# Retention attention feeding a mixture of experts: score products in half rows, and three loads that change place

## The chip, the cores and the metric

The kernel runs on one core of one Trainium2 chip. The metric is the time of one execution on the device in microseconds (us). For the kernel before, three runs took 440.48, 441.44 and 442.04 us; the median is 441.44.

A core has a matrix engine (TensorE, shown as PE for its products and PEld for the weight loads that go ahead of them), VectorE (DVE), ScalarE (ACT), GpSimd (POOL) and SyncE (SP). SP, ACT and POOL also ask for transfers between main memory and the core; sixteen DMA engines carry them. Each engine works through its own list of instructions in the order in which it is written, and waits at an instruction whose inputs aren't there.

## The reference

Two blocks, one after the other, all in 32-bit floats. The first is a retention recurrence over 4 batches, 8 heads, 768 tokens and heads of 64:

```python
gamma = 1.0 - 2.0 ** (-5.0 - np.arange(H))
scale = 1.0 / np.sqrt(D)
for t in range(S):
    state = gamma * state + np.einsum('bhd,bhe->bhde', k[:, :, t], v[:, :, t])
    y[:, :, t] = scale * np.einsum('bhd,bhde->bhe', q[:, :, t], state)
```

Its output, 3072 rows of 512, goes into a mixture of 8 experts in which each row is sent to the one expert with the highest logit:

```python
logits = x @ w_gate
expert_idx = np.argmax(logits, axis=1)
gate_w = softmax(logits)[arange(N), expert_idx]
for e in range(E):                       # the rows of expert e
    h = np.maximum(x_sorted[lo:hi] @ w1[e], 0.0)
    y_sorted[lo:hi] = h @ w2[e]
out = gate_w[:, None] * y                # back in the order of the tokens
```

w1 is 8 x 512 x 1024, w2 8 x 1024 x 512 (2 MB for each expert in each).

## The kernel before

**Attention in chunks.** The recurrence is worked in chunks of 128 tokens. Within a chunk there are products of scores (k against q, under a causal mask) and of the masked scores with v; across chunks a state of 64 x 64 per head is carried. The decay is put into q and v beforehand by element-wise products with a table (`scale_q`, `scale_v`: lines 606 and 611). There are STEPS = 12 steps (lines 906 on); a step handles one chunk for two batches, and steps 0 and 2 and so on (the even ones) begin a pair of chunks that share one load of q of 512 KB per batch. k and v are loaded per step and batch, 256 KB each. Step s does, in the order that is written by hand for every engine:

- asks for the loads of later steps (ACT for q; SP for k and v of step s + 3), and scales q and v for coming steps on POOL;
- `scores` for both batches (line 650). A tile `sc[j]` holds for one parity j of the head four pairs of heads. Each head's product is 64 x 128 x 128 and is split in two here, over c, so that a quadrant of 64 x 64 of the matrix engine is used by each: four products, two parities j and two halves c, fill the array. DVE masks them (line 655);
- products of the carried state with q (`with_state`, line 674, 64 x 64 quadrants);
- for the even following step, transposes of q (`turn_q`, line 617, copied by ACT, line 630, called from `ahead_q` in odd steps), and for every following step transposes of k (`turn_k`, line 617, copied by ACT, line 636, called from `ahead`);
- the rows of the step before are turned on DVE (`to_rows`, line 716) and stored by SP to `x_d` in main memory (`store`, line 723); logits (lines 734 to 745);
- the new state (`next_state`, line 687) and the products of masked scores with v (`within`, line 705), copied by ACT (lines 708 and 711).

**Loads at the start.** Before the loop SP asks for q, k and v of step 0, k of step 1, q and k of step 2, v of step 1 and v of step 2, in this order. v of step 1 is scaled partly by POOL in step 0 (batch 1) and partly by DVE in step 1 (batch 0). From step 1 on, ACT asks for one 512 KB load of q at the start of every step until step 8: the first batch of a pair in odd steps, the second in even ones.

**Routing beside attention.** From steps 5 and 9 on and after the last step, `place` works out which expert each token belongs to and its rank there, in pieces that are threaded into the steps (`WHEN`). After the second of them, in step 10, the rows known so far for expert 0 are gathered from `x_d` by POOL (`gather`, line 174) into `xs2[0]`. Right behind these gathers POOL sets one element of the tile for expert 0's w1 (line 839). As the load of that part of the tile writes the same element, SP can ask for it (line 158) only after the gathers have been issued. The load comes in two halves of 1 MB over the columns of w1, each called from step 10, with the store of step 9 between them.

**The experts.** `layer1` (line 233) runs expert 0's first layer for 256 rows, one block of 128 columns of w1 at a time; further routing is worked out between the blocks, and the remaining rows are gathered. From 148 us on the experts follow densely: most products are those of line 333.

Of the kernel before, what the change touches and what calls it, by code (L numbers as in the profile page):

```python
# [13 lines left out]
F32 = mybir.dt.float32  # L14
# [7 lines left out]
P = 128  # L22
# [31 lines left out]
def kernel(  # L54
# [11 lines left out]
    nc = tc.nc  # L66
    B, H, S, D = q.shape
# [85 lines left out]
        nc.sync.dma_start(w1t, w1v[:, ds(e, 1), :, :])  # L153
        return w1t

    def half_of_weights1(w1t, e, i):

        nc.sync.dma_start(w1t[:, :, :, ts(i, F // 2)], w1v[:, ds(e, 1), :, ts(i, F // 2)])

    def weights2(pool, e, parts=1):  # L160
        w2t = pool.tile([P, 1, FT, DM], F32, tag="w2t", name="w2t")
# [406 lines left out]
    with ExitStack() as actx:  # L568
# [19 lines left out]
        def load(nm, s, b, parts=1, by=nc.sync):  # L588
            m, b1, e = where[s]
            src = {"q": q, "k": k, "v": v}[nm]  # L590
            if nm == "q":
                to = att.tile([P, H, 2 * D], F32, tag=nm, name=nm, bufs=4)
                for part in (ts(i, H // parts) for i in range(parts)):
                    by.dma_start(to[:, part, :], src[2 * b1 + b, part, ts(m, 2 * P), :].rearrange(
                        "h (t e) d -> t h (e d)", e=2))
            else:
                to = att.tile([P, H, D], F32, tag=nm, name=nm, bufs=8)
                nc.sync.dma_start(to, src[2 * b1 + b, :, ts(2 * m + e, P), :].rearrange("h t d -> t h d"))
            raw[nm, s, b] = to

        def scale_q(s, b, by=nc.gpsimd, parts=1):
# [7 lines left out]
        def scale_v(s, b, by=nc.gpsimd):  # L609
            vs = att.tile([P, H, D], F32, tag="vs", name="vs", bufs=4)  # L610
            by.tensor_tensor(out=vs, in0=raw.pop(("v", s, b)), op=ALU.mult,  # L611
                             in1=inner(dec[:, ts(NC + 2 * where[s][0] + where[s][2], H)], D))
            raw["vs", s, b] = vs
# [28 lines left out]
        def scores(s, b):  # L642
            kT, qT = front.pop((s, b)), q_of(s, b)
            sc = [pairs_of("sc", 4, "sc") for _ in range(2)]
            am = [att.tile([P, HP, P], F32, tag=f"am{j}", name=f"am{j}") for j in range(2)]
            for a in range(HP):
                for c in range(2):
                    for j in range(2):
                        r = ts(j, D)
                        nc.tensor.matmul(sc[j][ts(c, D), a, :], lhsT=kT[r, a, ts(c, D)], rhs=qT[r, a, :],  # L650
                                         start=True, stop=True)

            def mask():
                for j in range(2):
                    nc.vector.tensor_tensor(out=am[j], in0=sc[j], in1=middle(causal[:, :], HP), op=ALU.mult)  # L655

            return am, mask
# [93 lines left out]
        def place(i):  # L751
# [82 lines left out]
            if i == NR - 2:  # L834
                head = inv[:, :, 0 : TC + HALF]
                src, far = sources(head, "_e")
                gather(xs2[0], src[:, 0:TC], range(HALF), 2 * NEXT[i + 1] * P)
                wa.append(first.tile([P, 1, DT, F], F32, tag="w1t", name="w1t"))
                nc.gpsimd.memset(wa[0][:, 0, 0, 0:1], 0.0)
                early.extend([head, far, src])  # L840

        def pad_ranks(at):
# [9 lines left out]
        def load_all(nm, s):  # L852
            for b in range(2):
                load(nm, s, b)
# [8 lines left out]
        load("q", 2, 0)  # L863
        load_all("k", 2)
        load("q", 2, 1)
        load_all("v", 1)
        load_all("v", 2)
        ctx.enter_context(tc.manual_schedule(engines={PE, ACT, POOL, DVE, SP}))
        xTa = first.tile([P, DT, EARLY], F32, tag="xTa", name="xTa")
# [32 lines left out]
        def step(s, at):  # L902
            for _ in range(WHEN.get(s, "").count(at)):
                next(rest, None)

        for s in range(STEPS):
            n = s + 2 + s % 2
            if 2 < n < STEPS:
                load("q", n, 1 - s % 2, by=nc.scalar)
            if s + 3 < STEPS:  # L910
                load_all("k", s + 3)
                if s == 7:
                    store(5)
                if s + 4 < STEPS:
                    load_all("v", s + 3)
            if s == 0:
                scale_q(2, 0)
                scale_q(2, 1)
                scale_v(1, 1)
            elif s + 2 < STEPS:  # L920
                if s % 2 and s > 1:
                    scale_q(s + 1, 1)
                for b in range(2):
                    scale_v(s + 1, b)
                if s % 2 == 0:
                    scale_q(s + 2, 0)
            if s in (1, 2):
                nc.gpsimd.memset(xs2[s % 2], 0.0)
            if s:
                am = [scores(s, b) for b in range(2)]  # L930
                am[0][1]()
                step(s, "m")
                if s + 2 != STEPS:
                    am[1][1]()
            y = outputs()
            if s + 1 == STEPS:
                logit = logits([s - 2, s - 1])
                rows_in_order()
            if where[s][0] or where[s][2]:
                with_state(s, y)  # L940

            def ahead():
                for b in range(2):
                    turn_k(s + 1, b)

            def ahead_q():
                if s % 2:
                    for b in range(2):
                        turn_q(s + 1, b)

            if s:
                if s + 1 < STEPS:
                    if s % 2:
                        logit = logits([s - 1] if s == 1 else [s - 2, s - 1])
                    ahead()
                reduce = logits_of(*logit) if s % 2 else lambda: None
                step(s, "p")
                if s + 2 == STEPS:
                    am[1][1]()
                    for b in range(2):  # L960
                        scale_v(s + 1, b)
                if s + 1 < STEPS:
                    ahead_q()
                to_rows(s - 1)
                reduce()
                if s == 1:
                    scale_v(1, 0, nc.vector)
                if s == NEXT[NR - 1] + 1:
                    half_of_weights1(wa[0], 0, 0)
                if s != 6:  # L970
                    store(s - 1)
                if s + 1 == STEPS:
                    wa.append(weights2(first, 0, 2))
                if s == NEXT[NR - 1]:
                    load_all("v", STEPS - 1)
                if s == NEXT[NR - 1] + 1:
                    half_of_weights1(wa[0], 0, 1)
                if s in NEXT:
                    rest = chain(rest, place(NEXT.index(s) - 1))
                step(s, "a")  # L980
            next_state(s)
            if s == 0:
                ahead()
            step(s, "b")
            if s + 1 == STEPS:
                pad_ranks(acc[:, NR - 1, 0:2])
            step(s, "r")
            within(s, y, am, early_rows if s + 1 == STEPS else lambda: None)
            step(s, "c")
# [319 lines left out]
```

## Time and profile before

| what | value |
|---|---|
| median of the runs (range) | 441.44 us (440.48 to 442.04) |
| profiled execution | 441.59 us, of which the span on the core is 439.9 us |
| PE busy in the span | 417.8 us (95%), 3979 products |
| PEld (weight loads) | 384.8 us (87%) |
| DVE, ACT, POOL busy | 244.1, 129.6 and 251.9 us |
| score products (line 650) | 768, 24.2 us busy |
| TensorE clock granted, mean | 0.994 |
| DMA over the span | 85.44 MB, 194 GB/s mean |

The span runs from the first to the last instruction on the core; the profiled execution is 1.69 us longer than its span. A 32-bit product stands in the profile as two records, and so does its weight load; that is why 32 calls of a step's scores show as 64. A row of a timeline gives start, time, engine, line, operation, output and inputs, the count of merged instructions, and in brackets how long the engine had been idle before it and what ended that. A row of the groups gives busy time and mean nanoseconds of one, and then the idle time before. Stretches give the busy time of each engine with the count of its instructions, then the granted clock, the mean busy share of the sixteen DMA engines and GB/s. A share a little over 1 can occur, since packets overlap on an engine.

### The profile page before, as it was taken

The page shows a single profiled execution, that of the slowest core. Times are in us where ns is not written, and L with a number is a line of the kernel's source. Part 1 is how long each engine was busy: PE and PEld are TensorE (multiplying, and loading weights), DVE is VectorE, ACT ScalarE, POOL GpSimd, SP SyncE. Part 2 cuts the span into 40 slices and gives each one's busy share as a digit, 9 for nine tenths or more (in the row PEclk, how much of TensorE's full clock was granted, in tenths as well). Part 3 has the DMA queues.
Part 4 walks back from the last instruction along what each step waited for, and adds up shares of the span by engine and source line. Part 5 has one row for each costly group of instructions (what it writes and reads, how often), then busy time and mean ns, then how long its engine had stood idle before and what let it go on. Part 6 is the DMA issues. An engine that isn't in the chain of part 4 may idle for free.

```text
span 439.9 us, 10496 instructions
## 1 busy us (share of the span) xinstructions
PE 417.8 (95%) x3979; PEld 384.8 (87%) x3979; DVE 244.1 (55%) x561; ACT 129.6 (29%) x288; POOL 251.9 (57%) x211
## 2 busy tenths in 40 slices
PE   7979999998899899999999999999999999999992
PEld 4869888887688858999999999999999999999681
DVE  4535579758578970453672575287168347635310
ACT  2445454452421212200322322032223214303340
POOL 4368536633137452989428936892893793496042
PEclk9999999999999999999999999999999999999997
DMA  9999899996991398743955693497589459321212
GB/s 202 241 220 255 204 239 271 218 215 137 299 298 47 110 397 265 209 151 78 391 145 155 245 291 89 127 343 192 160 286 272 98 159 353 74 84 40 62 70 80
DMA packets 122126, 85.44 MB, mean 194 GB/s; under 512 B 56970, under 2 KB 106122, under 8 KB 122000
## 3 DMA queue, kind: packets, MB, share of 16 engines
q1 hardware_dynamic: 108416, 67.15, 55.7%
q0 software_dynamic: 5120, 12.60, 8.6%
q10 hardware_dynamic: 8464, 4.24, 3.6%
q8 instruction: 52, 0.85, 0.9%
q14 instruction: 74, 0.61, 0.5%
HBM read 60.88 MB, written 14.68 MB: 172 GB/s over the span
## 4 chain that ended last, share of the span: by engine, by line
PE 79%; DMA 7%; issue 4%; DVE 3%; SPq 2%; POOL 2%; ACT 1%; POOLq 1%; DVEq 0%; ACTq 0%
PE p L333 52%; PE p L233 6%; PE y L705 4%; PE p L246 4%; PE sc L650 4%; DMA w1t<-in_moe_w_dram 2%; PE trk L617 2%; DMA v<-in_v_dram 2%; PE new L687 2%; PE trq L617 2%; PE hp L233 1%; PE y L674 1%; DVE xTa L217 1%; DMA q<-in_q_dram 1%; PE parts L734 1%
## 5 line engine op out<-in xcount | busy, mean ns | idle before, releaser
L337 DVE TENSOR_TENSOR q<-p,q 128x196 f32<-128x196 f32 (+5 forms) x72 | 24.0, 352 | 42.4 <-PE p L333 35.7
L655 DVE TENSOR_TENSOR am<-sc,causal 128x512 f32<-128x512 f32 x48 | 30.0, 683 | 20.8 <-PE sc L650 20.6
L522 POOL DMA_INDIRECT out_dram<-o,dst x26 | 25.9, 997 | 26.4 <-ACT o L1179 19.7
L611 POOL TENSOR_TENSOR vs<-v,dec 128x512 f32<-128x512 f32 x22 | 23.8, 1092 | 29.4 <-DMA v<-in_v_dram 18.2
L174 POOL DMA_INDIRECT xs<-x_d,src x28 | 31.1, 1112 | 14.7 <-issue 5.9
L333 PE MATMUL p<-t,w1t 128*128 128x196 f32 (+5 forms) x192 | 35.9, 330 | 0.0
L333 PE MATMUL p<-t,s 128*128 128x196 f32 (+5 forms) x192 | 35.8, 329 | 0.0
L333 PE MATMUL p<-g,w2t 128*128 128x216 f32 (+5 forms) x192 | 35.3, 337 | 0.0
L337 DVE TENSOR_TENSOR yT<-p,q 128x216 f32<-128x216 f32 (+5 forms) x36 | 12.9, 373 | 39.0 <-PE p L333 35.5
L333 PE MATMUL p<-g,z 128*128 128x196 f32 (+4 forms) x192 | 33.6, 328 | 0.0
L333 PEld LDWEIGHTS p<-g,w2t 128*128 128x128 f32 x192 | 33.4, 190 | 0.0
L337 DVE TENSOR_TENSOR hT<-p,q 128x196 f32<-128x196 f32 (+5 forms) x72 | 24.4, 352 | 16.0 <-PE p L333 15.4
L333 PE MATMUL p<-hT,w2t 128*128 128x196 f32 (+4 forms) x192 | 32.6, 328 | 0.0
L333 PEld LDWEIGHTS p<-t,w1t 128*128 128x128 f32 x192 | 32.4, 190 | 0.2 <-DVE q L337 0.2
L333 PEld LDWEIGHTS p<-t,s 128*128 128x128 f32 x192 | 32.5, 190 | 0.0
L1263 POOL COPY turn_of<-t 128x1 f32<-128x1 f32 x6 | 1.1, 184 | 54.3 <-DVE t L318 54.3
L333 PEld LDWEIGHTS p<-g,z 128*128 128x128 f32 x192 | 31.9, 190 | 0.0
L333 PEld LDWEIGHTS p<-hT,w2t 128*128 128x128 f32 x192 | 31.7, 190 | 0.0
L606 POOL TENSOR_TENSOR qs<-q,dec 128x512 f32<-128x512 f32 x22 | 22.7, 1056 | 12.9 <-DMA q<-in_q_dram 10.0
L705 PE MATMUL y<-am,vs 128*64 128x128 f32 x384 | 24.9, 275 | 3.1 <-issue 1.5
L650 PE MATMUL sc<-qT,kT 64*64 64x128 f32 x768 | 24.2, 273 | 1.4 <-ACT kT L636 1.4
L705 PEld LDWEIGHTS y<-am,vs 128*64 128x64 f32 x384 | 21.2, 137 | 4.9 <-issue 2.3
(231 smaller groups left out, 881.5 us busy)
## 6 DMA issues: line engine op xcount, KB each, us to landing
w1t<-in_moe_w_dram SPq DMA_DIRECT2D x7, 2048.0 KB
w2t<-in_moe_w_dram SPq DMA_DIRECT2D x7, 2048.0 KB
k<-in_k_dram SPq DMA_DIRECT2D x24, 256.0 KB
v<-in_v_dram SPq DMA_DIRECT2D x24, 256.0 KB
x_d<-xg SPq DMA_DIRECT2D x48, 128.0 KB
xs<-xs SPq DMA_DIRECT2D x96, 64.0 KB
o<-o SPq DMA_DIRECT2D x96, 64.0 KB
q<-in_q_dram ACTq DMA_DIRECT2D x8, 512.0 KB
```

The costliest lines, as they stand in the source:

```text
L174: nc.gpsimd.indirect_dma_start(out=xs[:, t, :], out_offset=None, in_=x_d[0:rows, :], in_offset=bass.IndirectOffsetOnAxis(ap=idx[:, t : t + ...
L233: nc.tensor.matmul(hp, lhsT=w1t[:, 0, dt, ts(f, P)], rhs=xT[:, dt, n0:n], start=(dt == 0), stop=(dt == DT - 1))
L246: nc.tensor.matmul(y[j * z : j * z + m, 0:c], lhsT=hT[:, f, t * P + r0 : t * P + r0 + m], rhs=w2t[:, 0, f, ts(j, c)], start=(i == 0), stop ...
L333: nc.tensor.matmul(columns(y, c), lhsT=a, rhs=b, start=start and i == 0, stop=i + 1 == len(terms), skip_group_check=True)
L337: nc.vector.tensor_tensor(out=to, in0=y, in1=plus, op=ALU.add)
L522: done = nc.gpsimd.indirect_dma_start(out=out[:, :], out_offset=bass.IndirectOffsetOnAxis(ap=idx[:, t : t + 1], axis=0), in_=o[:, t, :], i ...
L606: by.tensor_tensor(out=qs[:, e, part, :], in0=got[:, part, ts(e, D)], op=ALU.mult, in1=inner(dec[:, ts(2 * where[s][0] + e, H)][:, part], D))
L611: by.tensor_tensor(out=vs, in0=raw.pop(("v", s, b)), op=ALU.mult, in1=inner(dec[:, ts(NC + 2 * where[s][0] + where[s][2], H)], D))
L617: nc.tensor.transpose(tr[:, a, :], src[:, 2 * a : 2 * a + 2, :].rearrange("p h d -> p (h d)"), ident)
L650: nc.tensor.matmul(sc[j][ts(c, D), a, :], lhsT=kT[r, a, ts(c, D)], rhs=qT[r, a, :], start=True, stop=True)
L655: nc.vector.tensor_tensor(out=am[j], in0=sc[j], in1=middle(causal[:, :], HP), op=ALU.mult)
L705: nc.tensor.matmul(place_of(y, b, a, j), lhsT=vs[:, 2 * a + j, :], rhs=am[b][0][j][:, a, :], start=alone, stop=True, skip_group_check=True)
```

## The change

Four things are changed.

- **Scores.** The split over c goes: one product for each head, 64 rows of the array by all 128 columns. The output `sc[j][:, a, :]` is the same.
- **v of step 1.** SP no longer asks for it. ACT asks for both loads in step 0, behind the copies of k of step 1. Both are scaled by DVE in step 1, behind `reduce`; POOL's part in step 0 goes.
- **q.** The load of the first batch of a pair, asked for by ACT at the start of an odd step, moves behind `ahead_q` of the same step, that is behind the copies of the turned q. The second batch's load stays at the start of the even step.
- **w1 of expert 0.** The tile is made in step 9, and SP asks there for its first quarter of columns (512 KB), behind v of step 11 and with no wait for the gathers. POOL's element now lies in the second quarter, which SP asks for where it asked for the first half; the second half follows as before.

```diff
-    def half_of_weights1(w1t, e, i):
+    def part_of_weights1(w1t, e, cols):
 
-        nc.sync.dma_start(w1t[:, :, :, ts(i, F // 2)], w1v[:, ds(e, 1), :, ts(i, F // 2)])
+        nc.sync.dma_start(w1t[:, :, :, cols], w1v[:, ds(e, 1), :, cols])
...
-                nc.sync.dma_start(to, src[2 * b1 + b, :, ts(2 * m + e, P), :].rearrange("h t d -> t h d"))
+                by.dma_start(to, src[2 * b1 + b, :, ts(2 * m + e, P), :].rearrange("h t d -> t h d"))
...
             for a in range(HP):
-                for c in range(2):
-                    for j in range(2):
-                        r = ts(j, D)
-                        nc.tensor.matmul(sc[j][ts(c, D), a, :], lhsT=kT[r, a, ts(c, D)], rhs=qT[r, a, :],
-                                         start=True, stop=True)
+                for j in range(2):
+                    r = ts(j, D)
+                    nc.tensor.matmul(sc[j][:, a, :], lhsT=kT[r, a, :], rhs=qT[r, a, :], start=True, stop=True)
...
-                wa.append(first.tile([P, 1, DT, F], F32, tag="w1t", name="w1t"))
-                nc.gpsimd.memset(wa[0][:, 0, 0, 0:1], 0.0)
+                nc.gpsimd.memset(wa[0][:, 0, 0, F // 4 : F // 4 + 1], 0.0)
...
-        load_all("v", 1)
         load_all("v", 2)
...
-            n = s + 2 + s % 2
-            if 2 < n < STEPS:
-                load("q", n, 1 - s % 2, by=nc.scalar)
+            if s % 2 == 0 and 0 < s < STEPS - 2:
+                load("q", s + 2, 1, by=nc.scalar)
...
                 scale_q(2, 1)
-                scale_v(1, 1)
...
                     ahead_q()
+                if s % 2 and s + 3 < STEPS:
+                    load("q", s + 3, 0, by=nc.scalar)
                 to_rows(s - 1)
                 reduce()
                 if s == 1:
-                    scale_v(1, 0, nc.vector)
+                    for b in range(2):
+                        scale_v(1, b, nc.vector)
                 if s == NEXT[NR - 1] + 1:
-                    half_of_weights1(wa[0], 0, 0)
+                    part_of_weights1(wa[0], 0, ts(1, F // 4))
...
                 if s == NEXT[NR - 1]:
                     load_all("v", STEPS - 1)
+                    wa.append(first.tile([P, 1, DT, F], F32, tag="w1t", name="w1t"))
+                    part_of_weights1(wa[0], 0, ts(0, F // 4))
                 if s == NEXT[NR - 1] + 1:
-                    half_of_weights1(wa[0], 0, 1)
+                    part_of_weights1(wa[0], 0, ts(1, F // 2))
...
             if s == 0:
                 ahead()
+                for b in range(2):
+                    load("v", 1, b, by=nc.scalar)
```

## The prediction

> **What bounds the kernel now.** I read the table of stretches first, cut where the attention steps stream (27.97 to 82) and where the dense expert products begin (148).
>
> ```profile
> core 0: us, PE busy (x) PEld busy (x) DVE busy (x) ACT busy (x) POOL busy (x), PEclk, DMA share, GB/s
> 0.00:27.97 27.97, 21.35 (x332) 16.28 (x334) 11.51 (x24) 10.71 (x18) 11.69 (x28) 1.00 1.05 217
> 27.97:55.00 27.03, 26.28 (x617) 23.76 (x616) 14.96 (x25) 13.00 (x23) 18.92 (x18) 1.00 0.99 232
> 55.00:82.00 27.00, 26.30 (x560) 23.20 (x556) 21.94 (x51) 14.21 (x26) 12.66 (x16) 1.00 1.00 244
> 148.00:439.90 291.90, 283.05 (x1688) 271.01 (x1688) 146.96 (x327) 71.45 (x180) 181.91 (x119) 0.99 0.60 185
> ```
>
> From 148 us the matrix engine is 97% busy (283.05 of 291.90) on instructions that the change doesn't touch, so what it wins or loses before 148 moves the end one for one. From 28 to 82 two resources are full at once: PE (26.28 of 27.03) and the DMA engines (share 0.99 and 1.00). PE can run ahead only as far as loads have landed early. So I read next what PE waits for (total us, times, longest).
>
> ```profile
> PE new L687 <- DVE vs L611: 1.9, 1, 1.9
> PE hp L233 <- DMA w1t<-in_moe_w_dram: 1.5, 1, 1.5
> PE y L705 <- issue: 1.5, 2, 0.7
> PE y L705 <- DVE state L693: 1.2, 1, 1.2
> PE found L829 <- DVE here L813: 0.7, 1, 0.7
> PE new L687 <- POOL vs L611: 0.5, 1, 0.5
> PE y L705 <- DVE am L655: 0.5, 2, 0.3
> ```
>
> No wait is for a k that is still loading. v in step 1 costs 1.9 + 0.5, the first expert weights 1.5, and three waits of L705 cost 1.5 + 1.2 with no input to blame: "issue" names nothing, and the state that the third is put down to is not an operand of line 705. Their places in the timeline (the weight loads), and the stretches that they cut off:
>
> ```profile
> 51.88 0.85 PEld L705 LDWEIGHTS y<-am,vs 128*64 128x64 f32 x16 [0.99 <-issue]
> 69.66 1.07 PEld L705 LDWEIGHTS y<-am,vs 128*64 128x64 f32 x19 [0.85 <-issue]
> 88.54 1.28 PEld L705 LDWEIGHTS y<-am,vs 128*64 128x64 f32 x22 [1.48 <-DVE state L693]
> 33.90:51.88 17.98, 17.24 (x386) 15.39 (x382) 10.24 (x18) 9.02 (x16) 12.61 (x12) 1.00 0.97 232
> 51.88:69.66 17.78, 17.07 (x380) 15.18 (x381) 12.47 (x29) 8.00 (x15) 8.20 (x12) 1.00 1.02 248
> 69.66:88.54 18.88, 17.65 (x380) 15.71 (x379) 14.99 (x31) 8.45 (x15) 11.65 (x12) 1.00 1.00 229
> q8 instruction: 9, 0.15, 1.4%
> ```
>
> Between stalls PE starts 768, 761 and 759 matmuls and weight loads: a fixed count, not a fixed place in the step (the second stall falls 12 products into a half, the others at 16 and 10). The last row, of the DMA view from 33.9 to 88.54, has nine instruction transfers: 2288 instructions over 9 is 254 each, so a stall comes at every third block of some 254. I read this as PE running out of fetched instructions while the fetch queues in the full DMA engines. [...]
>
> **Part 1, scores as 64x128 products.** Each step issues 64 loads and 64 matmuls for scores (768 over 12 steps); after it 32 and 32. A step then has about 64 of its 380 PE instructions fewer.
>
> ```profile
> 45.30 1.74 PEld L650 LDWEIGHTS sc<-qT,kT 64*64 64x64 f32 x64 [0.17 <-ACT xT L708]
> 46.99 0.92 PEld L674 LDWEIGHTS y<-qT,state 64*64 64x64 f32 x32
> 48.09 0.86 PEld L617 LDWEIGHTS trk<-ident,k 128*128 128x128 f32 x8 [0.17 <-issue]
> L650 PEld LDWEIGHTS sc<-qT,kT 64*64 64x64 f32 x768 | 21.0, 133 | 3.6 <-ACT kT L636 1.9 <-ACT xT L708 1.0 <-issue 0.5
> L233 PEld LDWEIGHTS p<-xT,w1t 128*128 128x128 f32 x128 | 19.7, 190 | 2.2 <-issue 0.5
> L233 PE MATMUL p<-xTa,w1t 128*128 128x104 f32 x64 | 7.4, 276 | 0.3 <-DVE xTa L217 0.3
> ```
>
> The streaming itself should cost the same. Four quadrants share 1.74/16 = 0.109 us now, one full 128-column product of the transposes takes 0.86/8 = 0.108, and two row halves side by side would take that long too. Three costs are new. (a) A gap of 0.17 us stands wherever the tile shape changes (before 45.30 and 48.09) and none between scores and state products, both 64*64 today; 64*128 beside 64*64 adds one gap in steps 1 and 3 to 10: 9 x 0.17 = 1.5 us. (b) A 128-column weight load takes 190 ns against 133, bare once per step: 12 x 0.057 = 0.7. (c) Products with 104 columns and 128-column loads come every 7.4/64 = 0.116 us, although they stream less, so such loads can set the pace: up to 16 x 0.007 = 0.1 a step; between nothing and 1.3 I take half, 0.6. In steps 9 and 10 PE waits for DVE anyway (0.7 for `here`, 0.5 for `am`), which hides some 0.7. That is **+2.1 us** (bounds 0 and +3.5).
>
> Against it, with 17% fewer instructions a block lasts about 7.3 us in place of 6.1 (18.2 us over three), 1.2 us more for the same fetch. Stalls of 0.99 and 0.85 vanish, 1.48 shrinks to about 0.3, and I keep 0.2 for what a faster PE meets again: 3.32 - 0.5 = **-2.8 us** (bounds 0 and -3.3).
>
> [...]
>
> **Part 2, who asks for v of step 1, and the first q of a pair later.** All of it is queueing on full DMA engines.
>
> ```profile
> 14.32 2.60 SPq L594 DMA_DIRECT2D q<-in_q_dram  x1
> 16.96 7.85 SPq L598 DMA_DIRECT2D v<-in_v_dram  x4
> 17.46 0.38 ACTq L594 DMA_DIRECT2D q<-in_q_dram  x1
> 21.36 2.04 POOL L606 TENSOR_TENSOR qs<-q,dec 128x512 f32<-128x512 f32 x2 [2.91 <-PE trk L617]
> 22.04 0.22 DVE L745 TENSOR_REDUCE lg<-parts 128x16 f32<-128x64 f32 x1
> 25.22 0.69 DVE L611 TENSOR_TENSOR vs<-v,dec 128x512 f32<-128x512 f32 x1 [2.97 <-DMA v<-in_v_dram]
> 26.19 3.08 POOL L611 TENSOR_TENSOR vs<-v,dec 128x512 f32<-128x512 f32 x3 [2.78 <-DMA v<-in_v_dram]
> 34.65 2.05 POOL L606 TENSOR_TENSOR qs<-q,dec 128x512 f32<-128x512 f32 x2
> ```
>
> Today v of step 1 stands on SP's queue behind k and q of step 2, while ScalarE's q of step 4, asked at 17.46 and not read before 34.65, moves at the same time. After it ScalarE asks for v at about 16 (behind the two kT copies), and that q after the qT copies, near 25. v should be there when DVE is free at 22.3; two scalings of 0.69 end at 23.7, and the 0.69 added to DVE lies in its wait of 2.97. So PE's waits for vs go: 1.9 + 0.5 = 2.4. Late next is the second q of step 2, which POOL starts to scale at 21.36 and PE transposes right behind it: it shares the engines with v from the new request on. A q is 0.5 MB, 2.3 us at the 217 GB/s of that stretch; but from 17.46 the other q took such a share already, so new crowding is what lies between 16 and 17.46, 1.4 us, of which SP's queue keeps about a third: 0.9 late. That is **-1.5 us** (bounds: -2.4 with no slip, 0 with one of 2.3). ScalarE's copies lose at most two issues of 0.38, ahead of products that still run; DVE's two scalings have `am` of the next step behind them, which can't start before.
>
> The later q: four requests move behind ACT's qT copies of their step, with only the copies of x behind them. For the first, 34.65 less 25 leaves 9.6 us, where 17.2 were; I take nothing (bounds 0 and +2.3: a pair's two requests now follow close on each other, so the second can land a whole q later and POOL's `qs`, then PE, with it). SP loses two issues early, so k and v of the next steps are asked sooner.
>
> **Part 3, the first quarter of w1.**
>
> ```profile
> 106.65 1.25 POOL L174 DMA_INDIRECT xs<-x_d,src_e  x1 [6.42 <-DMA v<-in_v_dram]
> 109.20 0.12 POOL L839 MEMSET w1t<- 128x1 f32 x1
> 109.35 8.73 DMA w1t<-in_moe_w_dram
> 115.63 0.85 PEld L705 LDWEIGHTS y<-am,vs 128*64 128x64 f32 x16 [0.17 <-issue]
> 118.22 1.97 PE L233 MATMUL hp<-xTa,w1t 128*128 128x256 f32 x8 [1.49 <-DMA w1t<-in_moe_w_dram]
> SPq L158 <- POOL w1t L839: 6.6, 1, 6.6
> ```
>
> The first half (1 MB) is held until the memset behind the gathers and lands 8.73 us later; PE waits 1.49. A quarter asked at 102.7 (SP sits for 6.6 us before 109.35) lands by 111.5 even if it takes as long as the half, and PE wants it at 116.6. The second quarter is asked where the half was, is half as large, and is wanted two columns' products (1.97 each) later, near 121. **-1.5 us** (bounds 0 and -1.5). The quarter may slow the gathers that start at 106.65: 0.5 MB are 2.3 us, and 102.7 + 2.3 is 105, so I take nothing; at worst +2.3. Then everything to 148 follows PE's order, and no stage gets more bytes.
>
> **Sum:** -2.8 + 2.1 - 1.5 - 1.5 = -3.7 us. The profiled execution took 441.59 (span 439.9 and 1.7 around it), so 437.9; the median of the runs shown, 441.44, is 0.15 less: **437.7 us**.
>
> **Rivals.**
> - *The DMA engines hold the pace.* With a share of 0.97 to 1.00 from 28 to 100, PE's gains of parts 1 and 2 could end as waits for k. For it: the shares. Against: not one wait of PE is for k, and the instruction blocks saved ride the same engines. Only part 3 remains: 441.4 - 1.5 = 439.9. Chance 0.18.
> - *The stalls stay*, being something else or moving to other blocks. Then +2.1 - 1.5 - 1.5 = -0.9: 440.5. For it: faster PE work asks for blocks sooner; against: the count of 759 to 768. Chance 0.17.
> - *Slower: row halves don't run side by side.* Place: the 32 score products of a step. If each takes 0.108 us alone, a step's scores take 3.5 in place of 1.74: +1.7 in the nine PE-bound steps, 15.3, and 2.1 of part 1's own, less the other gains of 5.8: 11.6 more, 453. No row shows 64*128; against it, the quadrants now use both row halves at once. It decides once a quarter of a half's time (3.7 of 15.3) is not covered by the other half. Chance 0.07.
> - *No effect*, each gain taken back at the last gathers or by late q: 441.4. Chance 0.06.
>
> **How the numbers follow.** The forecast has 0.52. No change is within 0.3% (1.3 us: 440.1 to 442.8), about what this kernel's runs can tell. Faster: 0.97 x 0.52 + 0.6 x 0.18 + 0.25 x 0.17 = 0.65. Slower: 0.07, and 0.06 for the tails of the last three: 0.13. Same: 0.22. The range runs from 435.0 (-3.3 + 0.7 - 2.4 - 1.5 = -6.5) to 441.6 (no effect); the forecast's own is 436.2 to 439.4.
>
> **What would show it.** Scores x384 in the page, 64*128, a step's 32 loads near 1.8 us and a gap of 0.17 before L674; no "issue" wait of L705 over 0.5; L687 of step 1 without a wait for vs; hp at L233 without a wait for w1t. I am wrong if score groups take over 2.2 us a step, if k or the second q of step 2 appears among PE's waits with over 1 us, or if the early row copies wait for the gathers longer than now.

## The result, and the profile after

The changed kernel takes **442.93 us** (441.43 to 445.02, 22 runs) against 440.48 (436.67 to 445.62, 22 runs) of the kernel before: a ratio of 1.0076 with a 95% interval of 1.0057 to 1.0095, some 3 us slower. The ratios in this document count only fast runs, none of them more than 1.5% above the fastest of its kernel, so they differ a little from the quotients of the medians, which count every run. The forecast was 437.7, 3.7 us below the median shown with it (441.44). The profiled execution of after took 442.48 us (span 440.8).

Of PE's waits in the changed kernel (total us, times, longest), the largest and those from 20 us on:

```profile
PE y L672 <- ACT xT L706: 4.4, 1, 4.4
...
PE trq L617 <- POOL qs L606: 0.9, 2, 0.5
PE y L672 <- ACT xT L709: 0.5, 1, 0.5
PE trk L617 <- DMA k<-in_k_dram: 0.5, 1, 0.5
```

Every wait that the prediction wanted gone is gone: none for vs, none for w1t, no "issue" wait of the products (line 703 now). The scores are the 384 products that were expected, and their loads take 1.86 us a step; the groups' row (busy, mean ns of one):

```profile
L649 PEld LDWEIGHTS sc<-qT,kT 64*128 64x128 f32 x384 | 22.4, 188 | 3.5 <-ACT kT L636 1.9 <-ACT xT L706 1.0 <-issue 0.5
```

But the first row of the waits is new: 4.4 us for ScalarE's copy of x (L706), in step 1. The chain of waits from 14 to 36 us of the changed kernel tells what that copy waited for (start, length, what):

```profile
16.40 6.84 DMA v<-in_v_dram
23.24 0.02 issue
23.26 0.37 ACTq L598
...
23.68 0.59 ACT xT L706
```

SyncE asks for v of step 2 at 16.40; 6.84 us later that transfer has landed; and 0.02 us after it ScalarE's *request* for the second v of step 1 goes out. A request was waiting for somebody else's transfer. In the trace of the changed kernel the 322 DMA requests of SyncE and ScalarE report their ends on eight counters, which the first sixteen take in turn; the two requests for v each wait for the counter that they report on. The earlier transfer on the first one's, a k that SyncE asked for at 13.81, has its last update at 20.35, and the request goes out at 20.37; on the second one's it is the v asked for at 16.40, with 23.24 and 23.26. ScalarE's queue in that trace (the eight counters are 0 to 7):

```
kT <- trk      waits PE, ACT     (both k of step 1)
DMA v <- in_v  waits counter 5   (earlier user: SyncE's second k of step 2)
DMA v <- in_v  waits counter 7   (earlier user: SyncE's first v of step 2)
xT <- y L706   waits PE
xT <- y L709   waits PE          (x2, the second with no wait of its own)
```

ScalarE works in order, so the copies of x stood behind the two requests. In the timeline of the changed kernel:

```profile
17.84 1.86 PEld L649 LDWEIGHTS sc<-qT,kT 64*128 64x128 f32 x32 [0.17 <-issue]
20.37 3.27 ACTq L598 DMA_DIRECT2D v<-in_v_dram  x2
23.68 0.59 ACT L706 COPY xT<-y 128x512 f32<-128x512 f32 x1 [6.93 <-DMA v<-in_v_dram]
24.32 0.69 PE L672 MATMUL y<-qT,state 64*64 64x128 f32 x4 [4.42 <-ACT xT L706]
```

The two requests go out at 20.37 and 23.26, not at 16. Before, the same copy (L708 there), PE's state products (L674) and the scores of step 2 stand at:

```profile
16.50 0.59 ACT L708 COPY xT<-y 128x512 f32<-128x512 f32 x1 [0.34 <-PE y L705]
19.06 1.05 PE L674 MATMUL y<-qT,state 64*64 64x128 f32 x32
29.65 1.98 PE L650 MATMUL sc<-qT,kT 64*64 64x128 f32 x64
```

PE's state products need the buffer that this copy frees, and they start at 24.32 instead of 19.06. Behind the idle time stands a second loss, in the stretches of the changed kernel cut at PE's wait (us, PE, PEld, DVE, ACT, POOL, granted clock, DMA share, GB/s):

```profile
19.90:24.32 4.42, 0.00 (x1) 0.00 (x1) 1.62 (x3) 0.62 (x2) 2.11 (x3) 0.78 1.11 229
24.32:29.30 4.98, 4.48 (x45) 2.93 (x46) 1.30 (x2) 1.50 (x3) 3.68 (x3) 0.51 1.36 214
```

After the wait PE runs at half its clock (0.51) for 5 us (4.98). Step 2's scores then start at 34.62, against 29.65 before: 5.0 us late. At the dense expert products (L233) 0.5 is left (148.57 against 148.08), and 0.9 at the end of the span. The rest of the 5 us is made up mostly by the waits that this profile of before has up to there and that of the changed kernel hasn't: the stalls (3.3 us) and the wait for w1t (1.5). Other executions of before have less of them, as shown further down.

### The profile page after: what moved, and what is told of

Its sections match the earlier page's. It is cut to its first block, busy times and chain, and to the rows that moved or that the text cites. A ratio compares the mean times of both kernels' runs of the same rounds, so it can differ in the third digit from the quotient of the medians.

```text
span 440.8 us, 9729 instructions
## 1 busy us (share of the span) xinstructions
PE 420.9 (95%) x3595; PEld 387.2 (88%) x3595; DVE 244.3 (55%) x562; ACT 129.7 (29%) x288; POOL 247.3 (56%) x210
## 4 chain that ended last, share of the span: by engine, by line
PE 85%; DVE 4%; DMA 3%; issue 2%; SPq 2%; ACT 1%; POOL 1%; POOLq 1%; ACTq 0%; DVEq 0%
PE p L333 51%; PE p L233 6%; PE y L703 4%; PE sc L649 4%; PE p L246 4%; PE hp L233 3%; PE y L672 2%; PE trk L617 2%; PE trq L617 2%; PE new L685 2%; DMA v<-in_v_dram 2%; PE parts L732 1%; DMA q<-in_q_dram 1%; DVE xTa L217 1%; SPq L594 1%
## 5 line engine op out<-in xcount | busy, mean ns | idle before, releaser
L174 POOL DMA_INDIRECT xs<-x_d,src x28 | 29.0, 1035 | 13.7 <-issue 6.4
L333 PE MATMUL p<-t,w1t 128*128 128x196 f32 (+5 forms) x192 | 35.9, 330 | 0.2 <-DVE q L337 0.2
L333 PE MATMUL p<-t,s 128*128 128x196 f32 (+5 forms) x192 | 35.8, 329 | 0.0
L333 PE MATMUL p<-g,w2t 128*128 128x216 f32 (+5 forms) x192 | 35.3, 337 | 0.0
L333 PE MATMUL p<-g,z 128*128 128x196 f32 (+4 forms) x192 | 33.6, 328 | 0.0
L333 PEld LDWEIGHTS p<-g,w2t 128*128 128x128 f32 x192 | 33.4, 190 | 0.0
L333 PEld LDWEIGHTS p<-t,w1t 128*128 128x128 f32 x192 | 32.3, 190 | 0.5 <-DVE q L337 0.5
L333 PE MATMUL p<-hT,w2t 128*128 128x196 f32 (+4 forms) x192 | 32.7, 328 | 0.0
L333 PEld LDWEIGHTS p<-t,s 128*128 128x128 f32 x192 | 32.5, 190 | 0.0
L333 PEld LDWEIGHTS p<-g,z 128*128 128x128 f32 x192 | 31.9, 190 | 0.0
L333 PEld LDWEIGHTS p<-hT,w2t 128*128 128x128 f32 x192 | 31.7, 190 | 0.1
L611 POOL TENSOR_TENSOR vs<-v,dec 128x512 f32<-128x512 f32 x21 | 21.5, 1046 | 17.8 <-PE y L703 16.3
L649 PE MATMUL sc<-qT,kT 64*128 64x128 f32 x384 | 24.9, 279 | 1.4 <-ACT kT L636 1.4
L649 PEld LDWEIGHTS sc<-qT,kT 64*128 64x128 f32 x384 | 22.4, 188 | 3.5 <-ACT kT L636 1.9
L342 ACT COPY q<-p 128x216 f32<-128x216 f32 (+6 forms) x24 | 7.8, 331 | 57.4 <-issue 39.1
```

The source lines that it names most:

```text
L174: nc.gpsimd.indirect_dma_start(out=xs[:, t, :], out_offset=None, in_=x_d[0:rows, :], in_offset=bass.IndirectOffsetOnAxis(ap=idx[:, t : t + ...
L333: nc.tensor.matmul(columns(y, c), lhsT=a, rhs=b, start=start and i == 0, stop=i + 1 == len(terms), skip_group_check=True)
L649: nc.tensor.matmul(sc[j][:, a, :], lhsT=kT[r, a, :], rhs=qT[r, a, :], start=True, stop=True)
```

## The experiments

Beside the changed kernel's own, the runs come in four groups, each with runs of the kernel before (medians 440.47 for e1 to e4, 438.36 for e5 to e8 without e6b and e7b, 438.24 for e9 and e6b, 438.58 for e11 and e7b), so between groups only ratios are compared.

| kernel | median, us | ratio to before | 95% interval | clock in the profile |
|---|---|---|---|---|
| changed kernel | 442.93 | 1.0076 | 1.0057 to 1.0095 | 0.986 |
| e1 changed, v back at SyncE | 437.28 | 0.9938 | 0.9912 to 0.9964 | 0.995 |
| e2 before + v by ScalarE | 444.96 | 1.0109 | 1.0075 to 1.0142 | 0.988 |
| e8 changed, requests behind the copies | 440.82 | 1.0057 | 1.0031 to 1.0084 | 0.990 |
| e6 changed + 8 dummy products | 442.21 | 1.0096 | 1.0066 to 1.0126 | 0.994 |
| e6b changed + 4 dummy products | 440.59, one run | | | 0.994 |
| e5 changed, v asked by GpSimd | 437.83 | 0.9998 | 0.9974 to 1.0022 | 0.991 |
| e3 before + scores 64x128 | 438.33 | 0.9968 | 0.9939 to 0.9997 | 0.993 |
| e4 before + quarter of w1 | 440.89 | 1.0008 | 0.9975 to 1.0040 | 0.991 |
| e7 before + later q | 442.30 | 1.0106 | 1.0074 to 1.0139 | 0.996 |
| e7b the same, another execution | 442.91, one run | | | 0.991 |
| e9 scores and quarter | 437.77 | 0.9977 | 0.9951 to 1.0002 | 0.996 |
| e11 scores and later q | 436.15 | 0.9949 | 0.9923 to 0.9975 | 0.996 |

**Is it ScalarE's request for v?** In e1 the changed kernel gets v of step 1 as it was:

```diff
+        load_all("v", 1)                       # SyncE, ahead of v of step 2
         load_all("v", 2)
...
+                scale_v(1, 1)                  # GpSimd, in step 0
...
-                    for b in range(2):
-                        scale_v(1, b, nc.vector)
+                    scale_v(1, 0, nc.vector)
...
-                for b in range(2):
-                    load("v", 1, b, by=nc.scalar)
```

> The changed kernel with v of step 1 taken back to SyncE's queue and its second half to GpSimd's scaling; scores, the later q and the quarter of w1 stay. A (ScalarE's two v requests wait for earlier transfers and hold up the copies behind them, worth +5.0 us at step 1; the rest gains as forecast): 1.5 to 3 us below before, step 1's first copy of x again within 1 us of its products, no stretch with the clock at 0.5. B (the 64x128 products are what costs): level with the changed kernel or above before. C (the DMA engines hold the pace and hand every gain of PE back): 1.5 us below before at most, with waits of PE for k or v from 28 to 82 us.

e2 makes just the opposite edit to the kernel before.

> Before, with only the new way of v of step 1: ScalarE asks, VectorE scales both. A: 3 to 5 us above before, with ScalarE's first copy of x in step 0 held up by some 7 us and the clock down behind it. B: within 1 us of before. C: PE's late start lets loads get ahead and most of it comes back: 0 to 2 us above before.

A holds on both sides. e1 is 2.7 us faster than before (0.0062 of 440.5) and e2 is 4.8 us slower. e1's copy and step 2's scores, from its timeline, and e2's wait:

```profile
17.03 0.59 ACT L706 COPY xT<-y 128x512 f32<-128x512 f32 x1 [0.34 <-PE y L703]
28.10 2.06 PE L649 MATMUL sc<-qT,kT 64*128 64x128 f32 x32
```

```profile
PE y L674 <- ACT xT L708: 4.0, 1, 4.0
```

C falls with e2: a late PE did not get its time back.

**What makes up the loss: the copies, the clock, or v itself?** e8 moves ScalarE's two requests behind its three copies of step 0.

```diff
             if s == 0:
                 ahead()
-                for b in range(2):
-                    load("v", 1, b, by=nc.scalar)
...
             within(s, y, am, early_rows if s + 1 == STEPS else lambda: None)
+            if s == 0:
+                for b in range(2):
+                    load("v", 1, b, by=nc.scalar)
```

> The changed kernel with ScalarE's two requests for v of step 1 moved behind its three copies of x in step 0. They wait for the same two earlier transfers. A (what costs is what stands behind the requests in ScalarE's queue): the copies end near 18 again, the requests still go out near 20.4 and 23.3, the copy of lgT and the kT copies are the next that wait, to about 23.7, and the time is 4 to 5 us below the changed kernel, about 438.4. E (what costs is that v itself lands late or that the transfers collide): within 1.5 us of the changed kernel.

A's number was wrong. The copies were free, and step 2's scores started at 32.29, 2.3 us sooner than in the changed kernel but 4.2 later than in e1 (28.10); the time is only 0.2% below the changed kernel's, E's 1.5 us. e8's timeline names the two late things:

```profile
20.23 3.24 ACTq L598 DMA_DIRECT2D v<-in_v_dram  x2
23.94 0.44 PE L742 MATMUL parts<-ident,lgT 128*128 128x128 f32 x2 [1.77 <-ACT lgT L735]
29.18 0.69 DVE L611 TENSOR_TENSOR vs<-v,dec 128x512 f32<-128x512 f32 x1 [2.51 <-DMA v<-in_v_dram]
29.93 0.69 PE L685 MATMUL new<-vs,k 128*64 128x64 f32 x16 [1.53 <-DVE vs L611]
```

The requests wait as before, now with the copy of lgT behind them (1.77 us of PE); and of v, asked at 20.2 and 23.1, the second half lands only at 29.2. (The clock halves here too, from 24.25 to 27.66, but what PE waits for behind that stretch is v.) So here the wait of the requests cost twice: it held up the queue behind it (1.77 us of PE), and it made the transfer itself late (1.53 us of PE, behind `vs`). With the copies free, 2.6 of the 5.0 us that the changed kernel loses to before are still there (32.29 against 29.65).

e6 and e6b fill PE's wait with dummy products whose results nothing uses:

```diff
+            if s == 1:
+                for i in range(8):             # e6b: range(4)
+                    warm(512)
             if where[s][0] or where[s][2]:
                 with_state(s, y)
```

> The changed kernel with eight dummy products of 512 columns added on PE in step 1, ahead of the state products that wait for ScalarE's copy. They fill the wait and nothing uses their results. A1 (part of the loss is the halved clock that follows the wait): the granted clock stays at 1.00 from 20 to 30 us, the wait for the copy of x still ends near 24, and the time falls by 1.5 to 2 us against the changed kernel, to about 441. A2 (the wait alone is the loss, and what the clock takes is given back by loads that get ahead): within 0.5 us of the changed kernel.

> The changed kernel with half as many dummy products in ScalarE's wait of step 1, 3.6 us of them, so that they end before the copy of x does. Nothing uses their results. If the halved clock has a share of its own, the clock stays at 1.00, PE's work from the state products on runs about 2 to 2.9 us quicker, and what ends it next is the late v: step 1's L703 starts near 30.4 in place of 32.7. If not, L703 starts near 32.7 again.

A1's lower time did not come in e6 (1.0096). It overfilled: its dummies took 7.13 us and ended 3 us behind the copy, so its time decides little; that step 1 nonetheless reached `new` at 31.86, as in the changed kernel (31.79), was the hint. e6b's dummies end in time. Its stretches behind them, and in its timeline the products of step 1 and the next scores:

```profile
24.00:26.00 2.00, 1.00 (x24) 0.76 (x28) 0.58 (x1) 1.35 (x3) 2.00 (x3) 1.00 1.38 218
26.00:28.00 2.00, 2.00 (x33) 1.42 (x26) 0.72 (x2) 0.60 (x2) 1.97 (x2) 1.00 1.38 218
```

```profile
31.00 1.92 PE L703 MATMUL y<-am,vs 128*64 128x128 f32 x32
32.85 2.06 PE L649 MATMUL sc<-qT,kT 64*128 64x128 f32 x32
```

The clock stays at 1.00 and step 2's scores start at 32.85 in place of 34.62. The halved clock is worth **1.8 us** of the 6.5 between the changed kernel and e1 at that place (34.62 - 28.10). PE's waits for the copies are 4.4 + 0.5, against 0.7 that e1 waits for q there, which makes 4.2 of the other 4.7. (One run; the time, 440.59, agrees with the trace: the span is 1.9 below the changed kernel's.)

e5 lets GpSimd ask, whose 64 requests in the trace of the changed kernel report on eight other counters:

```diff
             if s == 0:
+                for b in range(2):
+                    load("v", 1, b, by=nc.gpsimd)
                 scale_q(2, 0)
...
-                for b in range(2):
-                    load("v", 1, b, by=nc.scalar)
```

> The changed kernel with v of step 1 asked for by GpSimd, ahead of its scalings of q, in place of ScalarE; GpSimd's requests name no earlier transfer to wait for. A: no wait on ScalarE, step 1's products start near 26 as with v back at SyncE, 436.5 to 438. E (v asked early collides with k and q of step 2): a wait of PE for qs or k of more than 1.5 us in step 1, 439 or more.

Half a hit for each. Nothing waits on ScalarE, and the time is in A's range, but against its own runs of before it is nothing won. E's collision is there, in its timeline and in a stretch behind it:

```profile
13.08 2.06 POOL L598 DMA_DIRECT2D v<-in_v_dram  x2
24.38 2.35 POOL L606 TENSOR_TENSOR qs<-q,dec 128x512 f32<-128x512 f32 x2 [5.78 <-DMA q<-in_q_dram]
25.77 0.66 PE L617 MATMUL trq<-ident,qs 128*128 128x128 f32 x4 [1.61 <-POOL qs L606]
```

```profile
28.00:30.00 2.00, 2.00 (x36) 2.00 (x34) 0.66 (x1) 0.09 (x1) 2.00 (x2) 0.50 0.98 214
```

Asked at 13, v pushes the second q of step 2 to 24.4 (22.1 in e1); PE waits for qs, and the halved clock follows here too. With the DMA engines full (share 1.15 and 1.10 in the stretches 17.84 to 19.90 and 19.90 to 24.32), what was asked early here came with something else late: the collision that the prediction had put at 0.9 is 1.6 us of PE here, though with v asked for at 13 and not at 16.

**The other terms.** e3 and e4 each do one part alone on the kernel before.

```diff
             for a in range(HP):
-                for c in range(2):
-                    for j in range(2):
-                        r = ts(j, D)
-                        nc.tensor.matmul(sc[j][ts(c, D), a, :], lhsT=kT[r, a, ts(c, D)], ...)
+                for j in range(2):
+                    r = ts(j, D)
+                    nc.tensor.matmul(sc[j][:, a, :], lhsT=kT[r, a, :], rhs=qT[r, a, :], ...)
```

> Before, with only the scores as 64x128 products. A: +2.1 - 2.8 = 0.7 us below before, no stall of L703 for fetched instructions, score groups about 0.1 us longer. B: 1 to 3 us above before. C: within 0.3 us of before, the stalls' time turned into waits for loads.

```diff
                 if s == NEXT[NR - 1]:
                     load_all("v", STEPS - 1)
+                    wa.append(first.tile([P, 1, DT, F], F32, tag="w1t", name="w1t"))
+                    part_of_weights1(wa[0], 0, ts(0, F // 4))
... (the memset and the other two parts as in the change)
```

> Before, with only the first quarter of expert 0's weights asked ahead of the early gathers. A and C: 1.5 us below before, hp without a wait for w1t. D (the quarter pushes the gathers or the last v back by as much): within 0.3 us of before, with hp's wait gone and a wait for the gathered rows or for v of the last step in its place.

The scores gain (1.4 us; the interval reaches from 0.1 to 2.7), as A had it, and no stall is left among e3's waits up to 148 us. The quarter shows no gain (the interval reaches from 1.1 us faster to 1.8 slower, so the 1.5 of A and C is out, a smaller gain isn't), though hp's wait was gone, and none of the waits that D named took its place. To see why, the kernel before was profiled twice more.

> The kernel before, profiled in another execution. A (PE's stalls for fetched instructions are there in each execution, at the same blocks): three waits of L705 near 51.9, 69.7 and 88.5 us again, 3.3 us in all, within 0.5. G (whether a block is late hangs on how its fetch falls among the loads): the stalls come at other blocks or are fewer, and the time goes with their sum. The same question for hp's wait of 1.5 for w1t and for a halved clock after the wait for v near 24 us.

> The same as in the look before it, a third execution: A has the three stalls in the same places, G has others.

G. Of the first of these executions (437.93 us, span 436.1), the weight loads that came late between 28 and 100 us, and PE's waits for v:

```profile
39.26 0.35 PEld L734 LDWEIGHTS parts<-xT,wg 128*32 128x32 f32 x9 [0.91 <-issue]
64.32 1.17 PEld L650 LDWEIGHTS sc<-qT,kT 64*64 64x64 f32 x41 [0.76 <-issue]
69.89 1.07 PEld L705 LDWEIGHTS y<-am,vs 128*64 128x64 f32 x19 [0.55 <-issue]
75.09 0.14 PEld L734 LDWEIGHTS parts<-xT,wg 128*32 128x32 f32 x4 [0.60 <-issue]
```

```profile
PE new L687 <- POOL vs L611: 1.5, 1, 1.5
PE new L687 <- DVE vs L611: 1.0, 1, 1.0
```

The same of the second (439.71 us, span 437.9):

```profile
46.84 0.97 PEld L650 LDWEIGHTS sc<-qT,kT 64*64 64x64 f32 x36 [0.49 <-issue]
53.01 0.85 PEld L705 LDWEIGHTS y<-am,vs 128*64 128x64 f32 x16 [1.24 <-issue]
```

```profile
PE new L687 <- DVE vs L611: 2.1, 1, 2.1
PE hp L233 <- DMA w1t<-in_moe_w_dram: 0.9, 1, 0.9
PE new L687 <- POOL vs L611: 0.5, 1, 0.5
```

The wait for v is there each time (2.5 and 2.6; 2.4 in the first profile). The stalls that the prediction read as instruction fetch, 3.3 us in the first profile, are 2.8 and 1.7 in these, at other lines and moments; hp's wait for w1t is 1.5, none and 0.9. The profile on which the prediction was built was the dearest of three in both.

e9 and e11 put parts together: e9 is the changed kernel without part 2, e11 the kernel before with the scores and the later q. e7 is the later q alone, e7b another execution of it.

```diff
-            n = s + 2 + s % 2
-            if 2 < n < STEPS:
-                load("q", n, 1 - s % 2, by=nc.scalar)
+            if s % 2 == 0 and 0 < s < STEPS - 2:
+                load("q", s + 2, 1, by=nc.scalar)
...
                     ahead_q()
+                if s % 2 and s + 3 < STEPS:
+                    load("q", s + 3, 0, by=nc.scalar)
```

> Before, with only a pair's first q asked for later. F (ScalarE's q at 17.46 is what holds v of step 1 back): step 1's waits for vs go or fall under 0.5 us, 1 to 2.5 us below before. As forecast (the move is worth nothing): within 0.5 us of before, with the waits for vs still near 2.4. The stalls for fetched instructions stay in both, near 3 us in all.

> The changed kernel without both edits of part 2: 64x128 scores and the quarter of w1 alone. If the later q is what brings v of step 1 early, the wait for vs (some 2.4 us in step 1) is back and the first scores of step 2 start near 29.5 in place of 28.1; if the gain of the later q lasts, the time is 1 to 1.5 us above that of the kernel with v back (ratio 0.996 to 0.998); if later waits for qs and k hand it back, as the forecast's nothing has it, the ratio is 0.994 again. PE has no stall for fetched instructions over 0.5 us up to 148 us.

> Before with only the later q, profiled in another execution. H (the two requests of a pair now follow each other, so q and k of steps 3 to 5 land later and PE waits for them): waits for qs and k of 2 to 3 us in all again, and scores of step 4 start later than before's 45.3 to 46.1 although step 2's start 1.4 us sooner. G (the stalls for fetched instructions and the wait for w1t differ from execution to execution, and the first profile of it caught many): those waits are smaller this time and the time falls with them, below 440.

> The 64x128 scores and the later q, without the quarter of w1 and with v of step 1 where it was. If the quarter is worth nothing here because hp does not wait for w1t once PE has no stalls, the ratio is that of the kernel with v back, 0.992 to 0.996. If the quarter is worth its 1.5 us, the ratio is 0.995 to 0.999, with hp's wait for w1t back.

e9's wait for v is back (1.6 us), its scores of step 2 start at 29.40, and its ratio is the one named for that case: beside the new scores the later q is worth some 0.3 to 0.4% (0.9977 against 0.9938 and 0.9949; the intervals overlap, so the traces, with step 2 starting 1.3 us sooner in e1 and e11, show it better than the times). It takes ScalarE's early q out of the way of v, F of e7. e11, without the quarter, is as fast as e1 with it (the intervals cover each other), and hp does not wait for w1t in it. So the quarter is worth nothing measurable beside the new scores; why hp's wait goes together with the stalls these runs don't show.

Alone, the later q costs 1.06%, and neither F nor the forecast's nothing said so. In e7b step 2's scores start at 28.50, 1.2 us ahead of before, as F had it; then, as H says, PE waits for the second q of step 4 and its clock halves (its waits, timeline and one stretch):

```profile
PE trq L617 <- POOL qs L606: 2.9, 5, 1.3
```

```profile
41.17 2.04 POOL L606 TENSOR_TENSOR qs<-q,dec 128x512 f32<-128x512 f32 x2
42.27 0.66 PE L617 MATMUL trq<-ident,qs 128*128 128x128 f32 x4 [1.30 <-POOL qs L606]
48.29 1.98 PE L650 MATMUL sc<-qT,kT 64*64 64x128 f32 x64
```

```profile
44.00:46.00 2.00, 2.00 (x38) 2.00 (x38) 0.21 (x1) 0.59 (x1) 1.21 (x2) 0.50 1.10 232
```

Step 4's scores start at 48.29, 3.0 late (45.30). In e7's own profile they start at 46.35 with a full clock, 1.0 late. That profile also shows 2.2 us of such stalls in the attention steps (0.80 at 52.73 and 1.36 at 71.21), hp's wait of 1.5 us for w1t and a stall of 1.5 us at L333. G's time below 440 did not come in e7b either (442.91), with 2.5 us of stalls (1.41 at 72.05 and 1.14 at 90.32) and no wait for w1t. Why e7 and e7b with the old scores wait 2.1 and 2.9 us for qs and e11 with the new ones 1.6 is not settled by these runs: two executions are too few to say how much of 1.06% is q's lateness, how much its halved clock and how much are stalls.

## Why the prediction was wrong

**The step that failed** is in part 2: "After it ScalarE asks for v at about 16" and "ScalarE's copies lose at most two issues of 0.38". The requests went out at 20.37 and 23.26, and ScalarE stood idle for 6.9 us ahead of its copies; PE waited 4.9 us for them, and its clock was halved from 22.41 to 29.24. Taken back alone (e1), the forecast's sign is right; done alone (e2), it costs 4.8 us. The prediction took a request as an instruction of 0.38 us that goes when its engine is free. A row for the opposite was among those it quoted: SyncE's four requests of v at 16.96 took 7.85 us. It read them as queueing of data on full engines, and not as a queue that an engine's next instruction would stand in. Its bounds for this edit ended at a gain of nothing. Even where the requests did not wait (e5), asking for v early gained nothing over e1 (0.9998 against 0.9938), since the second q of step 2 then came late: the gain of 1.5 us is in none of the runs.

**Part 1** was right in mechanism and near in size. A step's extra cost shows where no stall stands. The starts of scores in steps 8, 9 and 10, in the second repeat of before and in e11:

```profile
81.24 1.98 PE L650 MATMUL sc<-qT,kT 64*64 64x128 f32 x64
88.56 1.98 PE L650 MATMUL sc<-qT,kT 64*64 64x128 f32 x64
97.79 1.98 PE L650 MATMUL sc<-qT,kT 64*64 64x128 f32 x64
```

```profile
78.97 2.06 PE L649 MATMUL sc<-qT,kT 64*128 64x128 f32 x32
86.53 2.06 PE L649 MATMUL sc<-qT,kT 64*128 64x128 f32 x32
96.00 2.06 PE L649 MATMUL sc<-qT,kT 64*128 64x128 f32 x32
```

7.56 against 7.32, and 9.47 against 9.23: **0.24 us a step**, over nine steps 2.2 where 2.1 was forecast. The row halves do run side by side: a half starts a product every 0.116 us (1.86 by 16), less than one load's 188 ns. So the slower rival that was named (453 us) is out. The stalls went altogether up to 148 us, against "stalls stay", and nothing in the runs speaks against the reading of them as instruction fetch (the last section has the instruction transfers). Their size was that of one dear execution; the mean of three is 2.6. With 2.2 for the products, and without hp's wait for w1t (mean 0.8), which is gone in e3 as well, the rows make -1.2, and e3 measured -1.4.

**Part 2, the later q**, "I take nothing (bounds 0 and +2.3...)", was missed on both sides: beside the new scores it won some 0.3 to 0.4%, since v's way became free, and alone it cost 1.06%, which is 4.6 us and twice the bound. The wait that the prediction named as next, the second q of step 2, did come next: 0.7 us in e1.

**Part 3** was mis-sized: 1.5 us were one execution's wait, not the kernel's; others had 0.9 and none, and the measured ratio is 1.0008 (0.9975 to 1.0040). The rival "DMA engines hold the pace", which kept this part alone and let PE's gains go, falls with it and with e3, whose gain stayed.

**The sum** without the failed step would have been -2.8 + 2.1 - 1.5 = -2.2 us; e1 measured -2.7. Terms that were off in both directions made that agreement, so it proves the sum less than the single rows do. Also, "one for one" behind 148 us holds only within some 3 us: from the dense products to the end the profiles take from 291.2 (the first repeat of before) to 294.2 us (e3), with stalls at L333 a part of it.

**The version to keep** is e1 or e11: both beat both kernels, by 0.6% and 0.5% against before.

## What to carry to other kernels

A DMA request is an instruction with waits of its own (here two went out at 20.37 and 23.26, when earlier transfers had landed, and not at 16): before moving one to an engine that has other work, look which earlier transfer it must wait for, and what stands behind it in that engine's queue. Take the price of a stall from more than one execution, above all when the times before scatter by 2%. And a wait that can be predicted should be priced with what follows it: in e4 an idle PE of 2.2 us was followed by 3.4 us at half clock.

## What the runs showed of the hardware that was not expected

**Of two waits of about the same length, one was followed by a halved clock.** In the traces of before and of the changed kernel the granted clock changes at times that lie whole multiples of 3.413 us apart: full from 4.43 and half from 434.51 in before (126 times); full from 5.35, half from 22.41, full from 29.24 and half from 435.43 in the changed kernel (5, 2 and 119 times). In e4, whose edit acts only from 99.8 us on, the clock is full from 7.31 us on and half from 27.79, six times 3.41 later, to 31.21. Counted in stretches of that length from where the clock is first full, those around the wait for v in e4 and in before, and those around the wait for ScalarE's copy of x in the changed kernel, are:

```profile
24.38:27.79 3.41, 1.27 (x34) 1.16 (x36) 0.69 (x1) 0.58 (x1) 1.61 (x2) 1.00 1.00 197
27.79:31.21 3.42, 3.42 (x36) 3.09 (x32) 0.69 (x1) 0.59 (x1) 3.26 (x3) 0.50 1.12 234
```

```profile
21.49:24.91 3.42, 2.40 (x20) 1.92 (x18) 0.76 (x3) 3.17 (x6) 1.92 (x2) 1.00 1.13 217
24.91:28.32 3.41, 1.72 (x42) 1.61 (x44) 0.99 (x2) 0.00 (x0) 2.13 (x3) 1.00 0.91 204
```

```profile
19.00:22.41 3.41, 0.90 (x17) 0.71 (x14) 2.48 (x4) 0.00 (x0) 0.20 (x1) 1.00 1.01 239
22.41:25.83 3.41, 1.01 (x12) 0.60 (x16) 0.33 (x1) 1.75 (x3) 3.41 (x4) 0.50 1.32 228
25.83:29.24 3.41, 3.41 (x40) 2.27 (x33) 0.97 (x2) 0.37 (x1) 2.17 (x2) 0.50 1.36 213
```

The waits for v are about as long, 2.2 us in e4 and 2.4 in before. In e4 a single stretch holds the wait, with PE busy for 1.27 of 3.41 us, and in the stretch behind it PE has half its clock: the 32 products of L705 take 3.56 us there and 1.92 in before. In before the wait lies in two stretches, PE is busy for 2.40 and 1.72 us, and the clock stays at 1.00; it stays full in the two repeats as well, with waits of 2.5 and 2.6. In the changed kernel PE is busy for 0.90 and 1.01 us in the stretches from 19.00 and 22.41, and the clock is at half from 22.41 to 29.24. So in these three profiles half a clock followed the stretches with PE busy for 0.90 to 1.27 us and not those with 1.72 and 2.40; in e7b it followed about 1.77 us (3.41 less PE's waits of 1.30 and 0.34 ahead of 43.96, where the clock halves). How long a wait must be for it, and what sets where the stretches begin, these runs don't settle.

**The stalls differ from one execution to the next.** The same kernel had three of 0.85 to 1.48 us in one execution, four of 0.55 to 0.91 in another and two of 0.49 and 1.24 in a third. Each of these nine ends 1.35 to 1.58 us after a transfer of 16 KB of instructions has landed (in the first profile at 50.45, 68.27 and 87.05 us, and the stalls end at 51.88, 69.66 and 88.54). That a stall comes when the next block lands later than PE needs it is a reading of these times; no run shows the cause. How long such a transfer takes differs (0.88 to 2.74 us from 28 to 100 us in the three); what makes the difference is not shown. Of the nine profiles with 64x128 scores, with 17% fewer instructions in a step, none has such a stall between 28 and 148 us; of the seven with the old scores six have some (e2 has none). A wait of 0.8 to 1.5 us at L333 that no releaser explains, far behind, stands in e5 (0.8), e6 (1.0), e7 (1.5), e8 (1.4) and e9 (1.0) among others, and in none of the three of before.
